# Linear attention and two gated layers on one core: joining tail tiles from the streamed copy, and two early attention loads

## The chip, the cores and the metric

The kernel runs on one core of a Trainium2 chip. A core has TensorE (matmuls, PE in the profile), VectorE (DVE), ScalarE (ACT), GpSimd (POOL) and SyncE (SP), which here only issues DMAs; ScalarE issues some DMAs too. Each engine works off its own list of instructions in order. The metric is the device time of one execution in microseconds (us), as a median of several runs; lower is better.

## The reference, cut to what matters

q, k and v are [8 batches, 8 heads, 576, 64] in float32. The weights of both layers are float64 arrays of [512, 2048] and [2048, 512].

```python
kv  = einsum('bhsd,bhse->bhde', k, v)
o   = einsum('bhsd,bhde->bhse', q, kv)
x   = o / sqrt(mean(o * o, -1) + 1e-6) * g_norm      # -> [4608 tokens, 512]
h   = x @ w_in1;  g = 0 if h <= -1, h if h >= 1, else (h + 1)**2 / 4;  x = g @ w_out1
h   = x @ w_in2;  g = max(h, 0)**2;                                    out = g @ w_out2
```

## The kernel before

**Numbers.** Every float32 factor is split into a high and a low part (`split`, `split_halves`), and a product is three matmuls (high by high, high by low, low by high). A split is a copy on ScalarE (the high part) and a subtraction on VectorE (the low part). A float64 weight arrives as pairs of 32-bit words and is first narrowed to float32 (`narrow_w`).

**Tokens.** They are cut into nine blocks of 512 (eight of the first 512 rows of each batch, one of what is left over). The first layer of blocks 0 to 4 (`PLAIN = 5`) runs plainly: 16 steps per block, one for each 128 columns f of the first matrix. In a step `h_stage` makes `ph` (12 matmuls), VectorE and ScalarE make `u` and its split `gs`, and two steps later `out_stage` adds it into four `acc` banks (12 matmuls). `ph` has two banks, so `ph` of step f+2 needs `u` of step f. Everything else goes in pairs of blocks by a Strassen scheme (`in_phase`, `out_phase`), which needs sums of quarters of the weight matrices.

**Preparation.** Those sums are made while the plain blocks run. A unit (which, i) does it for the column groups i and i+8 of matrix `which` (0 the first, 1 the second) of both layers. For layer 2 `prep_load` brings the raw weights, `prep_narrow`, `prep_sums` and `prep_split` make the parts. For layer 1 `prep_join` adds the high and low parts of tiles that already exist (`j` in the trace), and `prep_sums` and `prep_split` follow. Every split tile `s` is sent to DRAM (`wsd`) by a store that ScalarE issues a little later. The work is hung on half steps by `hook(s, ...)`: s = 32 b is the start of block b. There are 16 units, one every 8 half steps.

**Tail tiles.** The second matrix of layer 1 has 16 tiles of 512 KB. Tiles 0 to 6 stay on the chip. Tiles 7 to 15 (`TAIL = 9`) are kept in DRAM and streamed in every block from the second on, by `load_tail`, into a ring of three (`wt` in the trace): a load is issued when the matmuls on the tile three before it are done. The unit of the second matrix with number i needs tile i+8 as well (and tile 7 for i = 7). It loads a second copy of that tile, `wf`, by `prep_load` into a slot of a ring of four (`prep_tile`) that the split tiles `s` use too, and joins it in place.

**Hosted attention.** Attention of batches 5 to 7 runs beside other work. `EARLY` is batch 5, pairs 0 to 2, in block 4. `HOSTED[0]` is (6,0), (6,2), (5,3), (6,1), (6,3), placed in the slots of the first `in_phase`. A job is a load of keys and values (`load_kv`) and q (`load_q`), then `kv_stage` (`pkv` in the trace, 40 small matmuls for two pairs), `t_stage`, `o_stage` and `r_stage`.

**Order.** A scheduler builds each engine's list from the order in which the program issues the work. SP's list carries nearly all loads, so one load that waits for its slot holds the loads behind it.

Of the kernel before, what the change touches and what calls it, by code (L numbers as in the profile page):

```python
# [10 lines left out]
F32 = mybir.dt.float32  # L11
# [66 lines left out]
def linear_attention_rms_two_mlps(  # L78
# [12 lines left out]
    nc = tc.nc  # L91
# [3 lines left out]
    P = 128  # L95
    NP = H // 2
    KD = DM // P
    NF = DFF // P
# [15 lines left out]
    wp = ctx.enter_context(tc.tile_pool(name="wp", bufs=1))  # L114
    TAIL = 9
    RING = 3
    NH = NF // 2
    NQ = NH // 2
    H2 = P * 2
# [13 lines left out]
    PLAIN = 5  # L133
    PAIRS = [(2, 0), (1, PLAIN), (2, 2), (1, PLAIN + 2), (2, 4), (2, 6)]
    EARLY = ((5, 0), (5, 1), (5, 2))
    HOSTED = {
        0: ((6, 0), (6, 2), (5, 3), (6, 1), (6, 3)),
        2: ((7, 0), (7, 2), (7, 1), (7, 3)),
    }
    hosted = [a for n in HOSTED for a in HOSTED[n]]  # L140
# [151 lines left out]
    def kept_whole(L, which, f):  # L292
        return wsd[L, which, f % NH // 2][:, f // NH * 2 : f // NH * 2 + 2, f % 2]
# [13 lines left out]
    raw_tags = itertools.cycle((NF - TAIL + RING, NF - TAIL + RING + 1))  # L307
    prep_tags = itertools.cycle(range(NF - TAIL + RING + 2, NF))

    def prep_tile(name, shape, dtype):  # L310
        return wp.tile(shape, dtype, tag=f"w1_{next(prep_tags)}", name=name)

    prep = {}

    def prep_load(L, which, i):
        if L == 1:
            for n in range(2):
                f = i + n * NH
                if which == 1 and f >= NF - TAIL:
                    t = prep_tile(f"wf_{f}", [P, 2, 2, H2], F32)  # L320
                    nc.sync.dma_start(t, kept_whole(1, 1, f))
                    prep[L, which, i, n] = t
            return
        for f in (i, i + NH):
            t = wp.tile([P, 2 * TB], I32, tag=f"w1_{next(raw_tags)}", name=f"raw2_{which}_{f}")
            src = w_src[2][which]
            if which == 0:
                nc.sync.dma_start(
                    t.rearrange("p (c f) -> p c f", c=KD),
                    src[:, 2 * f * P : 2 * (f + 1) * P].rearrange("(c p) f -> p c f", p=P),  # L330
                )
            else:
                nc.sync.dma_start(t, src[f * P : (f + 1) * P, :])
            w_raw[2, f, which] = t.rearrange("p (f two) -> p f two", two=2)
# [76 lines left out]
    def load_kv(b, hp):  # L411
        h0 = 2 * hp
        if b > 0:

            r = rests[turn[b, hp] % len(rests)]
            kvr[b, hp] = (r[:, 0], r[:, 1])
        both = None
        if (b, hp) in hosted:
            both = kv_ring.tile([P, 2, TB], F32, f"kv_{b}_{hp}")
        for n, src in enumerate((k, v)):  # L420
            if both is not None:
                t = both[:, n, :]
            else:
                pool, tag = (ep, "e") if (b, hp) == (0, NP - 1) else (st, "st")
                t = pool.tile([P, TB], F32, tag=tag, name=f"{'kv'[n]}_{b}_{hp}")
            rows = src[b, h0 : h0 + 2, :TB, :].rearrange("h (p r) d -> p h r d", r=MR)
            if n == 0:

                t = t.rearrange("p (r h d) -> p r h d", h=2, r=MR)
                nc.sync.dma_start(t, rows.rearrange("p h r d -> p r h d"))  # L430
            else:
                t = t.rearrange("p (h r d) -> p h r d", h=2, r=MR)
                nc.sync.dma_start(t, rows)
            kvm.setdefault((b, hp), []).append(t)
            if b > 0:
                rest = src[b, h0 : h0 + 2, TB:, :].rearrange("h p d -> p h d")
                nc.sync.dma_start(kvr[b, hp][n][:REM], rest)
# [14 lines left out]
    def load_first():  # L452


        left = wp.tile([REM, 2, H, D], F32, tag="w0_7", name="kvr0")
        qr = wp.tile([REM, H, D], F32, tag="w1_6", name="qr0")
        for hp in range(NP):
            load_kv(0, hp)
            heads = slice(2 * hp, 2 * hp + 2)
            kvr[0, hp] = (left[:, 0, heads, :], left[:, 1, heads, :])  # L460
            pool, tag = (ep, "e") if hp == NP - 1 else (st, "st")
            t = pool.tile([P, TB], F32, tag=tag, name=f"q_0_{hp}")
            t = t.rearrange("p (c h d) -> p c h d", h=2, c=MR)
            rows = q[0, 2 * hp : 2 * hp + 2, :TB, :].rearrange("h (p c) d -> p c h d", p=P)
            nc.sync.dma_start(t, rows)
            qs[0, hp] = [t[:, c] for c in range(MR)] + [qr[:, heads, :]]
            if hp == 1:
                for f in range(2):
                    load_w(1, f, 0)
            if hp == 0:  # L470
                for d, src in ((left[:, 0], k), (left[:, 1], v), (qr, q)):
                    nc.scalar.dma_start(d, src[0, :, TB:, :].rearrange("h p d -> p h d"))
                for j in range(2):
                    nc.scalar.dma_start(
                        gvec[j * D : (j + 1) * D, :], g_norm.rearrange("(d o) -> d o", o=1)
                    )
# [177 lines left out]
    def attention(base, every, order):  # L654

        slots = []
        for j, (b, hp) in enumerate(order):
            s = base + int(every * j)
            turn.setdefault((b, hp), len(turn))
            if b == 1:  # L660
                slots += [(max(0, s - 7), load_kv, b, hp), (s, kv_stage, (b, hp))]
            elif j % 2 == 0:
                two = order[j : j + 2]
                turn.setdefault(two[-1], len(turn))
                slots += [(max(0, s - 7), load_kv, *i) for i in two]
                slots.append((s, kv_stage, *two))
            slots += [
                (max(0, s - 7), load_q, b, hp),
                (s, t_stage, b, hp),
                (s + 3, o_stage, b, hp, 0),  # L670
                (s + 4, o_stage, b, hp, 1),
            ]
            if j == 0 and b < PLAIN:
                slots.append((s + 6, begin, b))
            slots.append((s + 6, r_stage, b, hp))
        if b < PLAIN:
            slots.append((2 * NF * b, store_xrem, b))
        return slots
# [425 lines left out]
    def hook(s, f, *a):  # L1104
        hooks.setdefault((s // 2, s % 2), []).append((f, a))
# [19 lines left out]
    for j, (w, f) in enumerate(kept):  # L1125
        hook(14 + 2 * j, keep_first, w, f)

    for j in range(2 * NH):
        which, i = j % 2, j // 2
        s0 = 2 * NF - 1 + 8 * j  # L1130
        for d, L, f, a in (
            (-6, 2, prep_load, ()),
            (0, 2, prep_narrow, (0,)),
            (1, 2, prep_narrow, (1,)),
            (2, 2, prep_sums, ()),
            (2, 2, prep_split, (0,)),
            (3, 2, prep_split, (1,)),
            (3, 2, prep_split, (2,)),
            (4, 2, prep_split, (3,)),
            (4, 1, prep_load, ()),  # L1140
            (6, 1, prep_join, ()),
            (7, 1, prep_sums, ()),
            (7, 1, prep_split, (2,)),
            (8, 1, prep_split, (3,)),
        ):
            hook(s0 + d, f, L, which, i, *a)

    last = 2 * (PLAIN - 1) * NF
    first_x = x2_jobs(0, Ring(*[(st, "st")] * 7))
# [4 lines left out]
        hook(last + t, load_w2)  # L1154
    in_pair = {}
    for n in HOSTED:
        for s, *job in sorted(attention(3, 6.5 if n == 0 else 7, HOSTED[n]), key=lambda j: j[0]):
            in_pair.setdefault((n, s), []).append(job)

    nc.scalar.preload_act_table_set("natural_log_exp_and_others")  # L1160
    load_first()
# [14 lines left out]
    for j in range(2):  # L1176
        s = slice(j * D, (j + 1) * D)
# [140 lines left out]
```

## Time and profile before

| what | value |
|---|---|
| median of 3 runs | 1588.13 us (1586.63 to 1588.62) |
| the profiled execution | 1591.16 us, span 1589.4 us |
| TensorE busy | 1545.9 us, 97% of the span |
| VectorE, ScalarE busy | 1197.8 us (75%), 930.4 us (59%) |
| DMA | 392.36 MB, mean 247 GB/s |

The profiled execution took 1591.16 us, of which the span that the profiler shows is 1589.4; both are a little above the median of the other runs. "Busy" is time in which an engine executes; a row of idle time names what ended the wait.

### The profile page before, as it was taken

How to read it: one execution, taken by the hardware profiler on the slowest of the kernel's cores; microseconds unless marked ns; L12 is line 12 of the kernel's file. 1: busy time of each engine (PE TensorE's matmuls, PEld its weight loads, DVE VectorE, ACT ScalarE, POOL GpSimd, SP SyncE). 2: the span in 40 equal slices, each digit the busy share in tenths (PEclk: the TensorE clock that was granted, in tenths of full speed). 3: DMA queues.
4: the chain of work that ended last, by engine and by line, in shares of the span. 5: the costliest groups of instructions: out<-in, count | busy, mean ns of one | idle time of the engine just before them, and what ended most of it. 6: DMA issues, size and time to landing. Idle time of an engine off the chain costs nothing.

```text
span 1589.4 us, 22383 instructions
## 1 busy us (share of the span) xinstructions
PE 1545.9 (97%) x7633; PEld 1271.6 (80%) x7633; DVE 1197.8 (75%) x2112; ACT 930.4 (59%) x1751; POOL 13.1 (1%) x30
## 2 busy tenths in 40 slices
PE   9999799999998889999999999999999999999999
PEld 5787687778876778888888888788888888888899
DVE  6975787887968847896888478878884587559666
ACT  5976665667756636764765366546753454346354
POOL 0000000000000000000000000000000000000000
PEclk9999999999999989999999999999999999999999
DMA  9676999889897887778777867687777676977796
GB/s 293 195 238 193 320 311 309 258 272 314 256 313 239 280 253 202 239 217 217 226 242 224 265 197 238 213 228 239 247 219 221 197 243 196 243 241 216 224 387 251
DMA packets 333090, 392.36 MB, mean 247 GB/s; under 512 B 197936, under 2 KB 223536, under 8 KB 332976
## 3 DMA queue, kind: packets, MB, share of 16 engines
q1 hardware_dynamic: 302080, 334.82, 69.9%
q10 hardware_dynamic: 30896, 56.11, 9.5%
q8 instruction: 61, 1.00, 0.2%
q14 instruction: 53, 0.43, 0.1%
HBM read 304.61 MB, written 86.25 MB: 246 GB/s over the span
## 4 chain that ended last, share of the span: by engine, by line
PE 82%; DVE 7%; DMA 7%; ACT 4%; issue 1%; SPq 0%; ACTq 0%; DVEq 0%
PE ph L881 30%; PE po L881 30%; PE acc L243 9%; PE ph L243 8%; DMA wsd<-s 3%; DMA wf<-wsd 1%; DMA wt<-wsd 1%; PE po L243 1%; PE pkv L490 1%; PE pr L612 1%; DVE s L190 1%; DVE t L810 1%; DVE u L708 1%; PE pwarm L1171 1%; DVE x L810 1%
## 5 line engine op out<-in xcount | busy, mean ns | idle before, releaser
L881 PE MATMUL ph<-x,ws 128*128 128x512 f32 (+1 forms) x2352 | 505.5, 375 | 0.9 <-DVE u L708 0.5
L881 PEld LDWEIGHTS ph<-x,ws 128*128 128x128 f32 x2352 | 418.1, 189 | 79.2 <-DVE e L937 0.8
L881 PE MATMUL po<-t,ws 128*128 128x512 f32 x2016 | 460.9, 390 | 0.3 <-DVE t L810 0.2
L881 PEld LDWEIGHTS po<-t,ws 128*128 128x128 f32 x2016 | 377.4, 188 | 81.0 <-DVE t L810 2.8
L810 DVE TENSOR_TENSOR t<-g,t 128x512 fp32r<-128x512 f32 (+1 forms) x336 | 215.9, 649 | 87.2 <-ACT t L222 84.6
L222 ACT CAST t<-g 128x512 fp32r<-128x512 f32 (+1 forms) x336 | 195.7, 590 | 116.4 <-PE po L881 58.6
L243 PE MATMUL ph<-x,w 128*128 128x512 f32 x960 | 245.8, 400 | 16.4 <-DVE u L708 14.8
L243 PEld LDWEIGHTS ph<-x,w 128*128 128x128 f32 x960 | 179.1, 191 | 60.2 <-DVE u L708 19.7
L243 PE MATMUL acc<-gs,w 128*128 128x512 f32 x528 | 135.7, 396 | 5.4 <-DVE gs L235 3.5
L958 ACT ACTIVATE g<-h 128x512 f32<-128x512 f32 (+1 forms) x120 | 70.7, 589 | 88.1 <-DVE h L947 88.0
L243 PEld LDWEIGHTS acc<-gs,w 128*128 128x128 f32 x528 | 97.9, 190 | 26.4 <-DVE gs L235 3.9
L937 DVE TENSOR_TENSOR e<-ph,e 128x512 f32<-128x512 f32 (+1 forms) x112 | 72.1, 650 | 58.6 <-PE ph L881 55.5
L243 PE MATMUL acc<-gs,wt 128*128 128x512 f32 x432 | 110.4, 403 | 2.1 <-DMA wt<-wsd 1.8
L947 DVE CUSTOM_DVE_ANT_0 h<-ph,e 128x512 f32<-128x512 f32 (+1 forms) x120 | 76.3, 637 | 47.4 <-PE ph L881 43.4
L243 PEld LDWEIGHTS acc<-gs,wt 128*128 128x128 f32 x432 | 83.6, 196 | 20.6 <-ACT u L229 2.2
L222 ACT CAST x<-xr 128x512 fp32r<-128x512 f32 (+1 forms) x98 | 57.5, 590 | 50.5 <-DVE xr L861 29.2
L222 ACT CAST gs<-u 128x512 fp32r<-128x512 f32 x80 | 49.9, 624 | 46.3 <-DVE u L708 29.6
L235 DVE TENSOR_TENSOR gs<-u,gs 128x512 fp32r<-128x512 f32 x80 | 54.8, 685 | 21.8 <-ACT gs L222 21.7
L708 DVE SCALAR_TENSOR_TENSOR u<-u,ph 128x512 f32<-128x512 f32 x80 | 54.5, 681 | 16.1 <-ACT u L229 15.8
L934 ACT COPY e<-ph 128x512 f32<-128x512 f32 (+1 forms) x56 | 30.8, 554 | 58.5 <-PE ph L881 51.6
L706 ACT ACTIVATE u<-ph,halfb 128x512 f32<-128x512 f32 x80 | 55.3, 691 | 13.4 <-PE ph L243 10.0
L810 DVE TENSOR_TENSOR x<-xr,x 128x512 fp32r<-128x512 f32 (+1 forms) x98 | 62.8, 646 | 0.0
(135 smaller groups left out, 1623.9 us busy)
## 6 DMA issues: line engine op xcount, KB each, us to landing
ws<-wsd SPq DMA_DIRECT2D x392, 512.0 KB, 4.1
wsd<-s ACTq DMA_DIRECT2D x96, 512.0 KB, 5.4
wt<-wsd SPq DMA_DIRECT2D x36, 512.0 KB, 5.8
raw<-in_moe_w_in_dram SPq DMA_DIRECT2D x32, 512.0 KB, 6.4
raw<-in_moe_w_out_dram SPq DMA_DIRECT2D x32, 512.0 KB, 5.7
xr<-x1d SPq DMA_DIRECT2D x36, 256.0 KB, 4.9
out_dram<-ov SPq DMA_DIRECT2D x142, 64.0 KB, 3.6
wsd<-w SPq DMA_DIRECT2D x17, 512.0 KB, 4.4
```

The costliest lines, as they stand in the source:

```text
L190: lo.tensor_tensor(t[:, :, 1, :], src, t[:, :, 0, :].bitcast(F32), ALU.subtract)
L222: return e.copy(dst, src)
L235: lo = engine(op + "_lo", phase).tensor_tensor(t[:, 1, :], src, t[:, 0, :].bitcast(F32), ALU.subtract)
L243: nc.tensor.matmul(dst, wt(a), xt(c), start=first and n == 0, stop=last and n == 2)
L706: nc.scalar.activation(u, ps, AF.Relu, bias=halfb, scale=0.5)
L708: nc.vector.scalar_tensor_tensor(u, u, 1.0, ps, op0=ALU.min, op1=ALU.max)
L810: engine2(op + "_lo").tensor_tensor(t[:, 1, :], src, t[:, 0, :].bitcast(F32), ALU.subtract)
L881: nc.tensor.matmul(ps, wt(a), xt(c), start=first and n == 0 and i == 0, stop=last and n == len(lhs) - 1 and i == 2, skip_group_check=True,)
L934: nc.scalar.copy(e[i, 1], bank)
L937: nc.vector.tensor_tensor(e[i, p], bank, e[i, 1], ALU.add)
L947: nc.vector._custom_dve(TENSOR_ADD_SAT, out=h, in0=bank, in1=add, s0=float("inf"), s1=0.0)
L958: nc.scalar.activation(g, h, AF.Square)
```

## The change

It has three parts. First, the units are put in another order: block n+1 now gets the units (0, 2n), (0, 2n+1), (1, n) and (1, n+4), at 32(n+1) - 4 + 2n + 0, 8, 16, 24 half steps; the last one starts one half step earlier, and what would fall behind block 4 is put in its last half step. By that order the second-matrix unit i meets the streamed tile i+8 of the same block, and `prep_join` reads that tile (into a small tile `j`) in place of a copy of its own. Only tile 7 of the last unit is still loaded as `wf`, into a slot of the ring for raw weights. Second, keys, values and q of the first two hosted pairs, (6,0) and (6,2), are loaded from half step 25 of block 4, the keys and values into the ring `st` (names `k_`, `v_`) and no longer into `kv_ring` (`kv_`). Third, the first hosted attention starts in slot 1 of the first `in_phase`, before in slot 3.

```diff
     def prep_load(L, which, i):
         if L == 1:
-            for n in range(2):
-                f = i + n * NH
-                if which == 1 and f >= NF - TAIL:
-                    t = prep_tile(f"wf_{f}", [P, 2, 2, H2], F32)
-                    nc.sync.dma_start(t, kept_whole(1, 1, f))
-                    prep[L, which, i, n] = t
+            if which == 1 and i >= NF - TAIL:
+                t = wp.tile([P, 2, 2, H2], F32, tag=f"w1_{next(raw_tags)}", name=f"wf_{i}")
+                nc.sync.dma_start(t, kept_whole(1, 1, i))
+                prep[L, which, i, 0] = t
             return
...
-        if (b, hp) in hosted:
+        if (b, hp) in hosted[2:]:
             both = kv_ring.tile([P, 2, TB], F32, f"kv_{b}_{hp}")
...
-    for j in range(2 * NH):
-        which, i = j % 2, j // 2
-        s0 = 2 * NF - 1 + 8 * j
+    units = []
+    for n in range(NQ):
+        for which, i, s in ((0, 2 * n, 0), (0, 2 * n + 1, 8), (1, n, 16), (1, n + NQ, 24)):
+            units.append((which, i, 2 * NF * (n + 1) - 4 + 2 * n + s))
+    units[-1] = (*units[-1][:2], 2 * NF * PLAIN - 7)
+    for which, i, s0 in units:
...
-            (4, 1, prep_load, ()),
+            (2, 1, prep_load, ()),
...
-            hook(s0 + d, f, L, which, i, *a)
+            hook(min(s0 + d, 2 * NF * PLAIN - 1), f, L, which, i, *a)
...
-        for s, *job in sorted(attention(3, 6.5 if n == 0 else 7, HOSTED[n]), key=lambda j: j[0]):
-            in_pair.setdefault((n, s), []).append(job)
+        for s, *job in sorted(attention(3 if n else 1, 7 if n else 6.5, HOSTED[n]), key=lambda j: j[0]):
+            if n == 0 and s == 0 and job[0] in (load_kv, load_q):
+                hook(last + 25, *job)
+            else:
+                in_pair.setdefault((n, s), []).append(job)
```

Three places in the engines' lists show it. In the names the numbers are block and step (`u_2_6` is `u` of block 2, step 6), tile (`wt_9`), or matrix and unit; the last number is a running one.

VectorE, block 2, where a second-matrix unit is joined; before:

```order
L708 SCALAR_TENSOR_TENSOR u_2_6_2983<-u_2_6_2983,ph_2_6_2970 128x512
L235 TENSOR_TENSOR gs_2_6_2989<-u_2_6_2983,gs_2_6_2989 128x512
L346 TENSOR_TENSOR wf_2967<-wf_2967 128x2x256
L366 TENSOR_TENSOR s_1_1_2_3087<-j_2_3024,wf_2967 128x256
L369 TENSOR_TENSOR s_1_1_2_3087<-s_1_1_2_3087,j_2_3024 128x256
```

and with the change:

```order
L706 SCALAR_TENSOR_TENSOR u_2_9_3197<-u_2_9_3197,ph_2_9_3184 128x512
L596 TENSOR_TENSOR s2lo_2_3208<-wk_3_2_3080,s_3_2_3168 128x576
L190 TENSOR_TENSOR s_1_1_3_3210<-s_2_1_1_3140,s_1_1_3_3210 128x2x256
L344 TENSOR_TENSOR j_9_3270<-wt_9_3176 128x512
L365 TENSOR_TENSOR s_1_1_1_3299<-j_1_3268 128x256
L364 TENSOR_TENSOR s_1_1_1_3298<-j_1_3268,j_9_3270 128x256
```

The join that read a private copy `wf` behind step 6 now reads the streamed tile `wt_9` behind step 9.

SP, end of block 4, the loads for the first hosted pairs; before:

```order
L303 DMA wt_14_5537<-wsd_1_3_113 128x2x512
L430 DMA kv_0_5659<-in_k_dram 128x8x64
L433 DMA kv_0_5659<-in_v_dram 128x2x256
...
L303 DMA wt_15_5584<-wsd_1_3_113 128x2x512
...
L430 DMA kv_2_5664<-in_k_dram 128x8x64
L321 DMA wf_5542<-wsd_1_3_113 128x2x512
L321 DMA wf_5544<-wsd_1_3_113 128x2x512
L433 DMA kv_2_5664<-in_v_dram 128x2x256
```

and with the change:

```order
L428 DMA k_0_5474<-in_k_dram 128x8x64
...
L303 DMA wt_10_5268<-wsd_1_1_111 128x2x512
L431 DMA v_0_5477<-in_v_dram 128x2x256
L428 DMA k_2_5480<-in_k_dram 128x8x64
...
L795 DMA ws_0_0_7_5085<-wsd_0_0_114 128x1024
L431 DMA v_2_5483<-in_v_dram 128x2x256
...
L303 DMA wt_13_5455<-wsd_1_2_112 128x2x512
...
L319 DMA wf_5546<-wsd_1_3_113 128x2x512
```

Three of the four loads of keys and values moved ahead of tile 11, the fourth (`v_2`) ahead of tile 13; one `wf` is left, behind tile 15.

TensorE, end of block 4, where `pkv` of the hosted pairs stands; before:

```order
L490 MATMUL pkv_0_5773<-kv_0_5659 64x64 x8
...
L243 MATMUL ph_4_15_5592<-x_4_0_3815,w_0_15_1154 128x512 x3
...
L490 MATMUL pkv_0_5773<-kv_2_5664 64x64 x8
```

and with the change:

```order
L243 MATMUL acc_4_3_4798<-gs_4_12_5440,wt_12_5394 128x512 x3
L488 MATMUL pkv_0_5706<-v_0_5477,k_0_5474 64x64 x8
L488 MATMUL pkv_0_5706<-rest_130 64x64 x2
L488 MATMUL pkv_0_5706<-v_2_5483,k_2_5480 64x64 x8
L488 MATMUL pkv_0_5706<-rest_129 64x64 x2
L243 MATMUL ph_4_15_5600<-x_4_0_3806,w_0_15_1154 128x512 x3
```

The part of the second pair moved up, from behind `acc` of step 14 to in front of `ph` of step 15.

## Rows read from the trace of the kernel before

**Rows 1.** The page, busy time of the engines.

```profile
PE 1545.9 (97%) x7633; PEld 1271.6 (80%) x7633; DVE 1197.8 (75%) x2112; ACT 930.4 (59%) x1751; POOL 13.1 (1%) x30
```

**Rows 2.** Windows: length, busy time (instructions) per engine, granted clock, DMA share, GB/s.

```profile
160.00:200.00 40.00, 30.59 (x160) 24.10 (x159) 31.11 (x60) 25.56 (x50) 0.81 (x2) 0.91 0.99 321
560.00:600.00 40.00, 36.02 (x164) 29.80 (x165) 19.69 (x35) 17.37 (x36) 0.00 (x0) 0.87 0.78 240
1100.00:1200.00 100.00, 100.00 (x443) 82.81 (x442) 81.50 (x131) 59.72 (x98) 0.00 (x0) 1.00 0.73 229
```

**Rows 3.** Timeline of TensorE: start, length, instructions, [idle before, what ended it].

```profile
170.34 5.43 PE L243 MATMUL ph<-x,w 128*128 128x512 f32 x12 [5.80 <-DVE u L708]
246.65 4.58 PE L243 MATMUL acc<-gs,wt 128*128 128x512 f32 x12 [1.81 <-DMA wt<-wsd]
272.08 2.88 PE L243 MATMUL acc<-gs,w 128*128 128x512 f32 x12
300.35 0.69 PE L490 MATMUL pkv<-v,k 128*64 128x64 f32 x16 [2.06 <-DVE t L530]
301.66 4.61 PE L243 MATMUL ph<-x,w 128*128 128x512 f32 x12
353.23 3.02 PE L243 MATMUL ph<-x,w 128*128 128x512 f32 x12 [1.69 <-DVE u L708]
451.41 3.01 PE L243 MATMUL ph<-x,w 128*128 128x512 f32 x12 [1.33 <-DVE u L708]
503.85 1.22 PE L243 MATMUL acc<-gs,w 128*128 128x512 f32 x2 [3.54 <-DVE gs L235]
528.44 3.01 PE L243 MATMUL ph<-x,w 128*128 128x512 f32 x12 [2.11 <-DVE u L708]
548.32 0.69 PE L490 MATMUL pkv<-kv 128*64 128x64 f32 x16 [2.06 <-DMA kv<-in_v_dram]
563.49 1.12 PE L490 MATMUL pkv<-kv 128*64 128x64 f32 x16 [4.62 <-DMA kv<-in_k_dram]
565.32 2.92 PE L881 MATMUL ph<-x,ws 128*128 128x512 f32 x6 [0.49 <-DVE u L708]
568.04 3.85 PE L243 MATMUL acc<-gs,wt 128*128 128x512 f32 x9
```

**Rows 4.** Timeline of VectorE: two `u` of block 1, two joins of `wf`, block 4's end.

```profile
150.51 0.69 DVE L708 SCALAR_TENSOR_TENSOR u<-u,ph 128x512 f32<-128x512 f32 x1 [0.43 <-ACT u L229]
169.61 0.68 DVE L708 SCALAR_TENSOR_TENSOR u<-u,ph 128x512 f32<-128x512 f32 x1
297.52 0.69 DVE L346 TENSOR_TENSOR wf<-wf 128x512 f32<-128x512 f32 x1 [4.96 <-DMA wf<-wsd]
502.50 0.69 DVE L346 TENSOR_TENSOR wf<-wf 128x512 f32<-128x512 f32 x1 [6.29 <-DMA wsd<-s]
545.68 0.65 DVE L861 TENSOR_TENSOR xr<-xr,xr 128x512 f32<-128x512 f32 x1
546.25 0.68 DVE L708 SCALAR_TENSOR_TENSOR u<-u,ph 128x512 f32<-128x512 f32 x1
```

**Rows 5.** All joins of the copy `wf`: idle time of VectorE before them.

```profile
  DMA wf<-wsd: 23.7, 5
  DMA wsd<-s: 6.3, 1
  DMA rest<-in_v_dram: 4.8, 1
```

**Rows 6.** Waits of SP's queue: total us, times, longest.

```profile
SPq L321 <- DMA wsd<-s: 17.7, 6, 5.4
```

**Rows 7.** DMA issues: count, KB each, median us from issue to landing.

```profile
wt<-wsd SPq DMA_DIRECT2D x36, 512.0 KB, 5.8
v<-in_v_dram SPq DMA_DIRECT2D x23, 256.0 KB, 4.9
```

**Rows 8.** The chain that ended last: one tail tile's transfer in block 1.

```profile
234.26 12.25 DMA wt<-wsd
```

## The prediction

> **What bounds the kernel now.** I start from the page: TensorE is busy for 1545.9 us of a span of 1589.4 [rows 1], so it sets the pace, and all that can be won without taking matmuls away is the 43.5 us in which it stands, and the stretches in which it runs at half its clock. The windows say where these lie. In the Strassen part (1100 to 1200 us) TensorE is busy all the time and the granted clock is 1.00; in the plain blocks there are windows of 40 us with 30.59 busy, and with a clock of 0.91 and 0.87 [rows 2]. So the timeline of TensorE is read for its idle times, one by one [rows 3]. [...]
>
> Then the reasons. Most rows name VectorE (`u`, `gs`, `t`), so VectorE's own waits are read. In front of the joins of the private copy `wf` it stood for 23.7 + 6.3 + 4.8 us [rows 5], 4.96 at 297 us and 6.29 at 502 us [rows 4]. These lead to TensorE's idle times at 300 (2.06), 353 (1.69), 451 (1.33) and 503 us (3.54): what TensorE waits for stands in VectorE's list behind such a join. And why was `wf` late? SP waited 17.7 us in six of the nine cases until the store of a split tile had freed the slot [rows 6]; only then did the transfer begin. The wait at 548 us and that at 563 us are for values and keys of the first hosted pairs themselves, which SP issues late, the second between the last two `wf`.
>
> **The change part by part.** All against the profiled execution, 1591.2 us.
>
> *Eight of nine loads of `wf` go.* With them go SP's waits for the slot, and VectorE's for the transfer. What TensorE lost behind these: at 300 us 2.06 + (4.61 - 2.88) = 3.8; at 353 us 1.7; at 451 us 1.3; at 503 us 3.5 [rows 3]. Together 10.3.
>
> *Hosted keys, values and q early.* The waits at 548 us (2.1) and 563 us (4.62, 0.49, then 2.92 for six in place of 1.44 and 3.85 for nine in place of 2.16, so 4.62 + 0.49 + 1.48 + 1.69 = 8.3) go: 10.4. The last `wf` pair, for which VectorE stood here too, becomes one load behind the last tail tile, in a slot of the raw ring, which its unit's narrowing frees.
>
> *What follows from these.* At 528 us 2.11 are waited for a `u` behind work that VectorE has piled up since the wait at 502 us; bounds 0 and 2.1, I take 1.0. At 246 us a tail tile needed 12.25 us [rows 8] while the next `wf` moved beside it at a DMA share near 1 (0.99 in the window before, [rows 2]); bounds 0 and 1.81 + 1.70 = 3.5, I take 1.0, since the copy was issued 5 us behind the tile. Removed in all: 10.3 + 10.4 + 2.0 = 22.7 us.
>
> *The joins now wait for streamed tiles.* A tail load is issued when the tile three before it is done, that is about one step (two times 2.88 us) ahead of the join's place in the list and two ahead of its matmuls. The median transfer is 5.8 us [rows 7], about that lead, so I take 0; bounds 0 and what the longest transfer would cost, under the rivals. What hides the join is then the step in between; without it VectorE's list stands still, and `u` with it.
>
> *A new wait in front of `ph` of step 15.* `pkv` of both pairs now stands there on TensorE. Three of its four loads are issued many steps ahead. The fourth, values of (6,2), gets the slot in `st` of a tile whose last reader is the last difference of x quarters (`xr`, L861 before); in the changed list that stands right behind `u` of step 13. Before, `u` of step 13 was done at 546.9 us [rows 4], when TensorE came to the same place (548.32 less 2.06: 546.3). The load then lands 4.9 us later [rows 7], and TensorE would stand for some 5.5 us, with the clock 8.6. But VectorE comes there earlier: it lacks the 6.29 us wait at 502 us, while TensorE lacks 3.54 and about 1.0; and in the changed list some 4 us of preparation (part of the last unit, which starts two half steps later, and a transpose) stand behind `u` of step 13 and no longer before. That is some 5.5 us less. Bounds 0 and 8.6; I take 3.0, since the estimate of what VectorE is ahead may be half wrong. Behind that load on SP are tail tiles 13 and 14, needed one and two steps later, so they are covered.
>
> *The units in other places.* VectorE has the same operations, but in other bunches. At the opening of block 1, the list before has 26 rows between `u` of step 3 and of step 4, which took from 151.2 to 169.6 us [rows 4] and cost TensorE 5.80 and (5.43 - 2.88) [rows 3], 8.4 in all. The changed list has a bunch of 32 rows, between `u` of steps 4 and 5, but two `gs` lie in the midst of it, and `u` of step 4 comes early. At the same pace it takes 4.2 us more; bounds -8.4 (no stall) and +4.2; I take 0. In block 4 the fullest two steps have 28 rows in place of 25, and blocks 2 and 3 get their bunches at other steps. A bunch that is a little too long costs what the small waits cost now, 1.3 to 1.7 us [rows 3]; bounds 0 and two in each of blocks 2 to 4 with the dearer figure, 10; I take one each, 4.5.
>
> *Sum.* 1591.2 - 22.7 + 0 + 3.0 + 0 + 4.5 = 1576.0 for a profiled execution. The median of the runs lies 3.0 below the profiled one, so **1573 us**. The bounds together (all good, all bad) give some 1591.2 - 20.7 - 5.6 - 8.4 - 3.0 = 1553 and 1591.2 - 20.7 + 8.6 + 4.2 + 10 - 3.0 = 1590.
>
> [...] The page shows TensorE at 97%, VectorE at 75% [rows 1]. [...]
>
> **The rivals.**
>
> *Hidden anyway, 1587 (within 0.2%).* TensorE is the engine that is full, and VectorE has as much to do as before (75%). Then each wait that goes comes back at the next bunch: VectorE is no longer held at 502 us, but the bunches at 170, 353 and 451 us are there in the new lists as well, and 20.7 us are given back as stalls of 1.3 to 5.8 each. For it: at 503 to 550 us VectorE worked with hardly a gap and TensorE still waited at 528 us. Against it: at 300 and 503 us VectorE itself stood idle for 4.96 and 6.29 us right before [rows 4]; that is no lack of capacity.
>
> *The values come late, 1580.* The load behind the difference of x costs its full 8.6 us in place of 3.0: 1573 + 5.6 = 1579, and with a step of TensorE waiting for tail tile 13 behind it about 1580. It is so if VectorE's lag at step 13 is the old one. For it: the rows at 545.68 and 546.25 us. Against it: the working above.
>
> *The joins wait, 1595 (slower).* Eight joins in the four blocks wait on VectorE for a streamed tile. If transfers take what the one at 234 us took, 12.25 us [rows 8], a join one step (5.8 us) behind the issue stands for 6.5 us, eight of them 52. Of the 34.8 us of idle time before `wf` [rows 5] TensorE lost 10.3 plus the 8.3 at 563 us, about half; so 26 us against the 20.7 that go: 1588 + 26 - 20.7 = 1593, and 1595 with a half-clock stretch. It decides from a mean wait of 5 us per join on, a landing of 11 us. Against it: the median is 5.8 us of 36 such transfers, and TensorE, which needs the same tiles a step later, waited for one only once, 1.81 us.
>
> **How the numbers follow.** The forecast, stalls behind `wf` and at the end of block 4 gone, 1562 to 1578: 0.66. Late values or dearer bunches, 1578 to 1584: 0.15. Hidden, 1585 to 1591: 0.10. Slower through the joins or the bunch of block 1, above 1591: 0.07. Better than 1562: 0.02. The range 1562 to 1587 leaves out about 0.02, 0.07 and half of the hidden case. This kernel's measurement tells a difference of about 0.2%, 3.2 us: faster 0.83, same 0.09, slower 0.08.
>
> **What would show it.** In the profile after, the groups of VectorE's waits should have one `wf` join left, and joins of `wt` without 5 us of idle time before them; TensorE's idle rows at the places of 300, 353, 451 and 503 us should be gone, and those in front of `pkv` at the end of block 4 be one, under 4 us, ended by a load of values. Block 1 should still have its stall of several us, one or two steps later. I am wrong if joins of `wt` show waits, if `pkv` waits over 6 us, or if the windows of blocks 2 to 4 show as much idle TensorE as now with VectorE busy.

## The result and the profile after

The changed kernel takes 1570.47 us (median of 4 runs, 1569.12 to 1574.38), beside 1588.38 for the kernel before on the same chip: a ratio of 0.9892 [0.9873, 0.9912], 17.9 us less. Its profiled execution took 1570.57 us with a span of 1568.8, that of before 1591.16.

The page of the changed kernel, its line of busy times [rows 1 for before]:

```profile
PE 1537.6 (98%) x7631; PEld 1268.9 (81%) x7633; DVE 1197.7 (76%) x2112; ACT 932.2 (59%) x1751; POOL 11.9 (1%) x30
```

TensorE stood for 31.2 us of the span (1568.8 less 1537.6), before for 43.5. The rest of the 20.6 us between the two spans is clock: the mean granted clock is 0.996 in place of 0.990, and TensorE's "busy" time for the same matmuls is 8.3 us less. The windows of the changed kernel (the columns as in [rows 2]):

```profile
160.00:200.00 40.00, 34.62 (x175) 27.11 (x174) 34.55 (x66) 27.54 (x57) 0.94 (x2) 0.91 0.99 308
240.00:480.00 240.00, 234.10 (x1195) 192.56 (x1194) 194.25 (x368) 165.67 (x331) 4.25 (x8) 0.99 0.86 272
520.00:560.00 40.00, 35.57 (x189) 28.68 (x189) 28.53 (x54) 21.17 (x41) 0.00 (x0) 1.00 0.97 300
560.00:600.00 40.00, 40.00 (x219) 33.35 (x218) 30.35 (x50) 25.95 (x52) 0.00 (x0) 1.00 0.71 218
```

The window from 560 us, which had stood at a clock of 0.87, is full and at a clock of 1.00. That at 160 us still has the clock of before, 0.91. TensorE's idle times behind 160 us in the changed kernel, from its timeline (those over 1 us; the columns as in [rows 3]):

```profile
171.51 2.10 PE L243 MATMUL acc<-gs,w 128*128 128x512 f32 x8 [2.21 <-DVE gs L235]
...
174.71 0.53 PE L243 MATMUL po<-qT,kvbd 128*128 128x288 f32 x2 [1.09 <-ACT qT L222]
...
176.84 1.33 PE L243 MATMUL po<-qT,kvbd 128*128 128x288 f32 x4 [1.60 <-DVE qT L569]
...
415.24 0.53 PE L243 MATMUL po<-qT,kvbd 128*128 128x288 f32 x2 [1.64 <-ACT qT L222]
...
472.93 0.53 PE L243 MATMUL po<-qT,kvbd 128*128 128x288 f32 x2 [3.50 <-ACT qT L222]
473.30 4.48 PE L243 MATMUL ph<-x,w 128*128 128x512 f32 x12
...
517.17 0.53 PE L610 MATMUL pr<-s2lo,ones 128*128 128x288 f32 x2 [1.44 <-DVE s2lo L596]
...
542.70 1.66 PE L879 MATMUL ph<-x,ws 128*128 128x512 f32 x6 [2.36 <-DVE u L706]
...
552.32 8.01 PE L879 MATMUL ph<-x,ws 128*128 128x512 f32 x34 [2.07 <-ACT ev L743]
...
636.36 0.53 PE L243 MATMUL po<-qT,kvbd 128*128 128x288 f32 x2 [1.93 <-ACT qT L222]
```

All waits of [rows 3] from 246 us on are gone; between 240 and 390 us there is no wait of 0.3 us or more. But there are new ones, at 415, 473, 517, 542, 552 and 636 us, of which that at 473 us costs 3.50 and 1.6 more (twelve matmuls in 4.48 in place of 2.88, at a granted clock of 0.62 from 473.3 to 477.8 us). What ScalarE, VectorE and the queue in which ScalarE issues its stores did before that wait:

```profile
471.27 0.37 ACTq L182 DMA_DIRECT2D wsd<-s  x1
471.69 0.63 ACT L229 ACTIVATE u<-u 128x512 f32<-128x512 f32 x1 [4.55 <-DMA xr<-x1d]
```
```profile
472.35 0.69 DVE L706 SCALAR_TENSOR_TENSOR u<-u,ph 128x512 f32<-128x512 f32 x1 [3.87 <-ACT u L229]
```

ScalarE stood for 4.55 us until it had issued a store, and VectorE stood behind it for 3.87; so this wait doesn't come from a full VectorE. VectorE's waits in front of joins, in the list of waits (total, times, longest):

```profile
DVE j L344 <- DMA wt<-wsd: 6.9, 4, 2.3
```

Four joins of streamed tiles wait, 6.9 us in all, where the private copies had cost 34.8 [rows 5]. SP's wait for the slot of a copy [rows 6] is gone.

### The profile page after: what moved, and what is told of

It reads as the page before. It is cut to its first block, busy times and chain, and to the rows that moved or that the text cites. A ratio compares the mean times of both kernels' runs of the same rounds, so it can differ in the third digit from the quotient of the medians.

```text
span 1568.8 us, 22366 instructions
## 1 busy us (share of the span) xinstructions
PE 1537.6 (98%) x7631; PEld 1268.9 (81%) x7633; DVE 1197.7 (76%) x2112; ACT 932.2 (59%) x1751; POOL 11.9 (1%) x30
## 4 chain that ended last, share of the span: by engine, by line
PE 77%; DMA 6%; DVE 2%; ACT 2%; SPq 0%; issue 0%; ACTq 0%; DVEq 0%
PE po L879 32%; PE ph L879 31%; PE ph L243 6%; PE acc L243 6%; DMA wsd<-s 3%; DMA wt<-wsd 1%; PE po L243 1%; DMA ws<-wsd 1%; PE pkv L488 1%; PE pr L610 1%; DMA rest<-in_v_dram 1%; DMA xr<-x1d 1%; DMA xr<-xpd 0%; ACT s L222 0%; DVE s L190 0%
## 5 line engine op out<-in xcount | busy, mean ns | idle before, releaser
L243 PE MATMUL acc<-gs,w 128*128 128x512 f32 x528 | 131.7, 394 | 4.5 <-DVE gs L235 2.2
L243 PE MATMUL acc<-gs,wt 128*128 128x512 f32 x432 | 106.2, 391 | 0.8 <-DMA wt<-wsd 0.8
L243 PEld LDWEIGHTS acc<-gs,wt 128*128 128x128 f32 x432 | 79.9, 188 | 17.6 <-DMA wt<-wsd 1.2
L235 DVE TENSOR_TENSOR gs<-u,gs 128x512 fp32r<-128x512 f32 x80 | 54.9, 686 | 20.8 <-ACT gs L222 20.6
```

Of the source, the lines that this page charges most:

```text
L235: lo = engine(op + "_lo", phase).tensor_tensor(t[:, 1, :], src, t[:, 0, :].bitcast(F32), ALU.subtract)
L243: nc.tensor.matmul(dst, wt(a), xt(c), start=first and n == 0, stop=last and n == 2)
```

## The experiments

Each has its own runs of the kernel before on the same chip, so ratios are compared. "The changed kernel" stands at 0.9892.

**1. Only the units.** Hosted loads and start as before.

```diff
-        if (b, hp) in hosted[2:]:
+        if (b, hp) in hosted:
...
-        for s, *job in sorted(attention(3 if n else 1, 7 if n else 6.5, HOSTED[n]), key=lambda j: j[0]):
-            if n == 0 and s == 0 and job[0] in (load_kv, load_q):
-                hook(last + 25, *job)
-            else:
-                in_pair.setdefault((n, s), []).append(job)
+        for s, *job in sorted(attention(3, 6.5 if n == 0 else 7, HOSTED[n]), key=lambda j: j[0]):
+            in_pair.setdefault((n, s), []).append(job)
```

> Only the new unit order and the joins from streamed tiles; the hosted keys, values and q are loaded where they were, and the first hosted attention starts in slot 3 as before. Theory (two separate groups of waits, about 10 us behind the private copies and about 8 to 10 us in front of the small key-value matmuls at the end of block 4): the first group goes, the second stays, 1578 to 1580 us, and the rows of TensorE at 500 us and before have no wait for a join of a private copy, while the matmuls of keys and values still wait for a load. Rival A (the units are all of it): 1571. Rival B (the early loads are all of it): 1588.

1567.18 us, 0.9869 [0.9854, 0.9885]. That is rival A, and no less than the whole change. At the end of block 4 its timeline of TensorE has one wait for a hosted load left:

```profile
532.26 1.12 PE L488 MATMUL pkv<-kv 128*64 128x64 f32 x16 [2.16 <-DMA kv<-in_v_dram]
```

The pair (6,2), for which TensorE had stood 4.62 us and more at 563 us [rows 3], is in time, though its loads are hung where they were. So the theory of two separate groups of waits fell.

**2. The early loads without the units:** the kernel before with the last block of the change's diff, so with its start in slot 1 too, and `hosted[2:]`.

> The kernel before with only the early loads of the first two hosted pairs and the start in slot 1; units, order and private copies as before. Theory: the waits in front of the key-value matmuls at the end of block 4 go, those behind the private copies at 300, 353, 451 and 503 us stay: 1578 to 1581 us; the two parts then add up to the whole change. Rival A (the units are all of it): 1588. Rival B (the early loads are all of it): 1571.

1588.55 us, 1.0007 [0.9996, 1.0018]: nothing, for the two parts together. The waits in front of `pkv` did go; what came is in the timelines of TensorE and VectorE of this kernel:

```profile
506.56 0.80 PE L243 MATMUL acc<-gs,w 128*128 128x512 f32 x1 [5.58 <-DVE gs L235]
...
562.88 0.61 PE L243 MATMUL po<-qT,kvbd 128*128 128x288 f32 x1 [3.25 <-ACT qT L222]
...
656.29 0.53 PE L243 MATMUL po<-qT,kvbd 128*128 128x288 f32 x2 [1.38 <-ACT qT L222]
```
```profile
503.84 0.69 DVE L346 TENSOR_TENSOR wf<-wf 128x512 f32<-128x512 f32 x1 [6.43 <-DMA wf<-wsd]
...
560.14 0.69 DVE L346 TENSOR_TENSOR wf<-wf 128x512 f32<-128x512 f32 x1 [3.20 <-DMA wf<-wsd]
...
564.59 0.69 DVE L346 TENSOR_TENSOR wf<-wf 128x512 f32<-128x512 f32 x1 [2.10 <-DMA wf<-wsd]
```

TensorE now waits at the end of block 4 for `qT`, whose work stands on VectorE and ScalarE around the join of the last pair of copies. Without the keys' wait the copies' own wait is what ends last. The wait at 656 us, with a clock of 0.89 from 650 to 665 us, is not in the kernel before; it comes with the start in slot 1 (experiment 7). So this run gives the sum of the two parts, and what the early loads alone are worth in the old order was not measured.

**3. The change with the private copies kept.** The old `prep_load`, hung at 4 half steps.

```diff
-            if which == 1 and i >= NF - TAIL:
-                t = wp.tile([P, 2, 2, H2], F32, tag=f"w1_{next(raw_tags)}", name=f"wf_{i}")
+            for n in range(2):
+                f = i + n * NH
+                if which == 1 and f >= NF - TAIL:
+                    t = prep_tile(f"wf_{f}", [P, 2, 2, H2], F32)
...
-            (2, 1, prep_load, ()),
+            (4, 1, prep_load, ()),
```

> The changed kernel, with the unit order and the early loads, but the units of the second matrix load their private copy of the tail tile again (nine loads of 512 KB into the slots that the split tiles use) and join that. Theory (the private copy, its wait for a slot in SP's list and VectorE's wait for it are what cost): some 10 us come back, 1578 to 1582, with waits of VectorE of 4 us and more in front of joins of the copy. Rival (the places of the units are what gains, the copy is harmless): 1571, within 2 us of the changed kernel.

1604.67 us, 1.0104 [1.0089, 1.012]. More than expected came back, 34 us over the changed kernel: in the new order the copies cost more than in the old (21.2 us, experiment 5). Of its list of waits and of VectorE's timeline:

```profile
DVE wf L346 <- DMA wf<-wsd: 46.2, 7, 10.5
```
```profile
343.69 0.69 DVE L346 TENSOR_TENSOR wf<-wf 128x512 f32<-128x512 f32 x1 [9.33 <-DMA wf<-wsd]
```

**4. The copies loaded but not read.** As 3, but the joins take the streamed tiles. There are seven such loads, not the eight of the expectation (the last unit has none).

```diff
+            elif which == 1:
+                t = prep_tile(f"wx_{i}", [P, 2, 2, H2], F32)
+                nc.sync.dma_start(t, kept_whole(1, 1, i + NH))
```

> As the kernel with the private copies kept, eight loads of 512 KB into the same slots at the same places, but nobody reads them: the joins take the streamed tiles, as in the changed kernel (tile 7 of the last unit apart). The loads are then only traffic and a place in SP's list that waits for a slot. Theory (what costs is that VectorE's list stands still behind the join): 1571 to 1574, at most 3 us above the changed kernel. Rival C (SP's list that stands still, or the traffic, makes streamed tiles and other loads late, and that is the cost): 1577 or more, and waits of TensorE or VectorE for streamed tiles.

1575.23 us, 0.9922 [0.9904, 0.994]: 4.8 us over the changed kernel, with the same slots. SP's waits for them and VectorE's for joins:

```profile
SPq L323 <- DMA wsd<-s: 6.3, 4, 4.4
```
```profile
DVE j L347 <- DMA wt<-wsd: 7.4, 4, 3.1
```

Between the theory's 3 and the rival's 7; the intervals of this and the changed kernel overlap. SP's waits for the slots were much the same in experiment 3, 7.0 us. So of the 34 us some 29 come only when VectorE's joins read the copies (nine there, seven loads here), and some 5, not clear of the noise, from the traffic and SP's place.

**5. The old order without copies.** The nine joins read tiles that lie on the chip, so the sums of those tiles are other ones.

```diff
-            for n in range(2):
-                f = i + n * NH
-                if which == 1 and f >= NF - TAIL:
-                    t = prep_tile(f"wf_{f}", [P, 2, 2, H2], F32)
-                    nc.sync.dma_start(t, kept_whole(1, 1, f))
-                    prep[L, which, i, n] = t
...
-                w = (wi[L, f] if which == 0 else wo[L, f]).bitcast(F32)
+                w = (wi[L, f] if which == 0 else wo[L, f if f < NF - TAIL else f % (NF - TAIL)]).bitcast(F32)
```

> The kernel before with its own unit order and its own hosted loads, but no private copy at all: the nine joins of tail tiles read a tile that lies on the chip (tile 1 for 8, 2 for 9 and so on), so the sums of these tiles are of other values; the work of VectorE is the same. Theory (the private copies are what cost, in either order; the 8.3 us in front of the key-value matmuls at 563 us were theirs as well, since the loads stood behind the last pair of copies in SP's list): 3.8 + 1.7 + 1.3 + 3.5 + 8.3 = 18.6 us go, about 1569 to 1573. Rival (the new order gains by itself, a better spread of VectorE's work): 1578 or more.

1565.61 us, 0.9858 [0.9837, 0.988], 21.2 us less than before. The rival falls: the order itself gains nothing. (Nine transfers are gone with them; in experiment 4 seven unread ones cost some 5 us.) Its window of blocks 2 to 4, and behind it the same window of the kernel before:

```profile
240.00:480.00 240.00, 239.67 (x1219) 197.54 (x1219) 200.53 (x380) 169.02 (x341) 3.29 (x8) 1.00 0.90 287
```
```profile
240.00:480.00 240.00, 230.94 (x1157) 187.51 (x1156) 190.08 (x361) 159.93 (x321) 6.15 (x8) 0.99 0.90 285
```

With the old list of VectorE and no copy to wait for, TensorE loses 0.3 us in 240; the changed kernel, in the new order, loses 5.9 there (the window above). What is left of this kernel's end of block 4 and of its block 1:

```profile
170.01 4.59 PE L243 MATMUL ph<-x,w 128*128 128x512 f32 x12 [5.04 <-DVE u L702]
...
198.94 2.47 PE L243 MATMUL acc<-gs,wt 128*128 128x512 f32 x5 [4.13 <-DMA wt<-wsd]
...
528.28 0.69 PE L484 MATMUL pkv<-kv 128*64 128x64 f32 x16 [1.60 <-DMA kv<-in_v_dram]
541.02 0.69 PE L484 MATMUL pkv<-kv 128*64 128x64 f32 x16 [2.20 <-DMA kv<-in_v_dram]
```

The two waits for hosted loads are 3.8 us here, 10.4 in the kernel before; both loads and starts are as before. So 6.6 of the 10.4 belonged to the copies: 2.9 of waits, the rest clock and the 0.49 behind.

**6. Joins two half steps sooner,** `(4, 1, prep_join, ())` for `(6, ...)`.

> The changed kernel with each unit's join two half steps (one step of TensorE, 5.8 us) earlier in the lists, half a step behind the issue of the tile's load in place of one and a half. Theory (a join that meets its tile too early holds VectorE's list, as the private copies did): eight joins wait some 4 to 6 us each, about half of it reaches TensorE, 1585 to 1595. Rival (VectorE has slack for it, since TensorE is the full engine): 1571, within 3 us of the changed kernel.

1573.03 us, 0.9906 [0.9888, 0.9923]. It doesn't tell the theories apart, since the scheduler put the joins in VectorE's list behind the same `u` as in the changed kernel (only that of the last unit moved, by one row). The rival that joins wait was thus not tried beyond the waits that the changed kernel has.

**7. Early loads, start in slot 3.** The changed kernel with `attention(3, ...)` for `attention(3 if n else 1, ...)`.

> The changed kernel with the hosted attention started in slot 3 as before; only the early loads of keys, values and q stay as changed. The kernel with the units alone took 1567.2, the changed one 1570.5. If the start in slot 1 is what loses the 3 us (its VectorE work meets the last unit and the first difference tiles): 1567. If the early loads lose them (transfers beside the last tail tiles): 1570 to 1571.

1565.46 us, 0.9862 [0.9843, 0.9881]. The waits at 552 us (2.07) and 636 us (1.93 and 0.51) are not in its timeline, that in front of `ph` is:

```profile
541.26 2.08 PE L879 MATMUL ph<-x,ws 128*128 128x512 f32 x6 [2.75 <-DVE u L706]
543.14 4.12 PE L243 MATMUL acc<-gs,wt 128*128 128x512 f32 x12
```

So the start in slot 1 loses some 4.5 us by these rows, and the clock falls behind the wait at 636 us too (0.87 from 630 to 640 us, here 1.00). That wait, 1.9 to 2.4 us in two pieces, is in the traces of all kernels that start in slot 1 (2, 3, 4 and 6 as well, at 637 to 671 us) and of none that starts in slot 3. The one at 552 us is less certain: in experiment 6 it is 0.35. The early loads lose nothing that shows against experiment 1, and gain nothing clear of the noise. The intervals of this kernel and of the changed one still touch, so the loss is read from the traces and not shown by the times.

**8. Stores by GpSimd,** in the kernel of experiment 1: `nc.gpsimd.dma_start(dst, src)` for `nc.scalar.dma_start(dst, src)` in `pay`.

> The kernel with the units alone (1567.2), with the stores of split tiles and of x1 quarters issued by GpSimd, which is idle, in place of ScalarE. Theory (what is left at 175, 416 and 473 us, 3.4 us at the longest, is ScalarE's list standing in the issue of a store): these rows go, 1560 to 1564. Rival (the transfers themselves are late in a full DMA, whoever issues them): 1567. A third: GpSimd issues later or more slowly, slots come free later, 1570 and more.

1586.11 us, 0.9993 [0.9979, 1.0006], the third way. The table of DMA issues of this kernel (xcount, KB, median us to landing) and a row of its list of waits; behind them the same of experiment 1:

```profile
wsd<-s POOLq DMA_DIRECT2D x96, 512.0 KB, 6.6
```
```profile
ACT s L222 <- DMA wsd<-s: 24.3, 11, 4.1
```
```profile
wsd<-s ACTq DMA_DIRECT2D x96, 512.0 KB, 5.2
```
```profile
ACT s L222 <- DMA wsd<-s: 12.9, 7, 2.9
```

A store lands later (6.6 us against 5.2), and ScalarE waits twice as long (24.3 us against 12.9) to write a split tile into a slot that such a store must free. That this is all of the 19 us is not shown: the scheduler made other lists, and VectorE's joins wait longer than in the changed kernel (6.9):

```profile
DVE j L344 <- DMA wt<-wsd: 12.8, 3, 7.2
```

**9 and 10. Two attempts at the waits that are left,** on the kernel of experiment 7: the first differences of x quarters two to four half steps later (9), the units of block 1 two half steps later (10).

```diff
-    when = [2, 3, 3, 4, 5, 6, 7, 8, 7, 9, 9, 10, 11, 12, 13, 14]
+    when = [2, 4, 5, 5, 6, 7, 8, 9, 7, 9, 10, 11, 12, 13, 14, 15]
```
```diff
-            units.append((which, i, 2 * NF * (n + 1) - 4 + 2 * n + s))
+            units.append((which, i, 2 * NF * (n + 1) - (2 if n == 0 else 4) + 2 * n + s))
```

> The kernel with the units and the early loads but the start in slot 3 (0.9862 of before, 1565.5), with the first differences of x quarters, which begin in block 4, hung two to four half steps later. What is to go is the row at 472 us (2.27 to 3.5 us and a stretch at half clock; ScalarE stands there in the issue of a store while the x quarters move and the DMA share is 1.0). If VectorE's bunch there (18 rows between two u) and those transfers are the cause: 1561 to 1563. If the store is slow for another reason: 1565. If the later differences collide with the end of block 4: 1568.

> The same kernel with the units of block 1 hung two half steps later. VectorE's longest bunch there, 33 rows between u of step 4 and step 5, falls apart into bunches of 7 to 15. Theory (the stall of 5.2 us at 170 to 179 us and the half clock behind it come from that bunch, not from the transfers): 5.2 us and 3 to 4 us of half clock go, 1557 to 1560. Rival (the transfers of the raw weights and the store that ScalarE issues hold it, DMA share 0.99): 1564 to 1566.

9 took 1565.63 us (0.9865 [0.9843, 0.9887]), 10 took 1565.89 (0.987 [0.985, 0.9889]): both the same as experiment 7. Single traces scatter: up to 440 us the lists of TensorE, VectorE and SP in 9 are those of 7, yet TensorE is busy for 71.21 us at a clock of 0.94 from 160 to 240 us, there 71.89 at 0.98. In 9 the wait at 472 us fell to 0.37, but others of 0.96 and 0.65 came at 498 and 513. In 10 the waits of 171 to 179 us went, and these came (TensorE's timeline):

```profile
193.00 0.73 PE L243 MATMUL ph<-x,w 128*128 128x512 f32 x2 [1.93 <-DVE u L706]
198.90 4.60 PE L243 MATMUL acc<-gs,wt 128*128 128x512 f32 x12 [1.72 <-DMA wt<-wsd]
213.86 5.46 PE L243 MATMUL acc<-gs,wt 128*128 128x512 f32 x12 [3.34 <-DMA wt<-wsd]
```

**11. The copy sooner,** in the kernel before: `(2, 1, prep_load, ())` for `(4, ...)`.

> The kernel before with each private copy hung two half steps earlier and, in the ring of slots, behind the first split tile of its unit in place of the last, so that it takes a slot that is freed earlier. The joins move up in VectorE's list by up to a step as well. Theory A (it is SP's wait for the slot that makes the copy late): the waits in front of the joins shrink to a third and the time is 1570 to 1576. Theory B (a copy of 512 KB beside the raw weights and tail tiles is late wherever it is issued, and the join in the list goes with it): 1585 to 1595.

1580.27 us, 0.9953 [0.9939, 0.9967], between the two. The lists of waits of VectorE and of SP (for before see [rows 5, 6]):

```profile
DVE wf L346 <- DMA wf<-wsd: 13.6, 4, 4.7
```
```profile
SPq L321 <- DMA wsd<-s: 1.9, 2, 1.5
```

SP's wait fell from 17.7 to 1.9 us, VectorE's from 34.8 to 13.6, the time by 8.4. So issuing the copy earlier, into a slot that is freed earlier, took away a good part of its lateness; the two weren't tried apart. What holds the time up is not shown to be the transfer alone, since ScalarE now waits longer for the slots of split tiles (11.7 before):

```profile
ACT s L222 <- DMA wsd<-s: 26.0, 14, 5.8
```

**12. First-layer stores closer together,** on the kernel of experiment 7: `hook(14 + 5 * j // 4, keep_first, w, f)` for `14 + 2 * j`.

> The kernel with the units, the early loads and the start in slot 3 (0.9862 of before), with the stores of the first layer's own tiles hung closer together, so that they end in the middle of block 1's first third and not at its end: some 14 transfers of 256 KB leave the stretch 160 to 235 us, where the DMA share is 1.0, for 80 to 160 us, where it is 0.36 to 0.83. The scheduler also makes VectorE's longest bunch of block 1 25 rows in place of 33. When the units of block 1 alone were moved, TensorE's wait of 5.2 us at 171 us came back as 7 us of waits at 193 to 214, five of them for tail tiles. Theory (in block 1 the transfers are the limit, and a stall that is moved comes back while they are): 1557 to 1561. Rival (VectorE's bunches are the limit in block 1, wherever the transfers lie): 1564 to 1567.

1573.65 us, 0.9909 [0.9889, 0.993]: worse, and neither theory had it. Its timeline of TensorE:

```profile
148.42 1.90 PE L243 MATMUL ph<-x,w 128*128 128x512 f32 x5 [2.50 <-DVE u L706]
177.80 2.50 PE L243 MATMUL ph<-x,w 128*128 128x512 f32 x5 [3.35 <-DVE u L706]
```

The stall of block 1 is there, in other places and one of them earlier. What sets block 1's loss stays open.

## Why the prediction was right, and where its steps were not

The forecast was 1573 us, the time is 1570.5; the sum for the profiled execution was 1576.0, it took 1570.6. The mechanism that the sum rests on, VectorE's list standing behind a join for a private copy, is shown by experiments 3 to 5. But several terms were wrong, and their errors nearly cancel: the copies were worth about twice what was booked for them, the early loads hardly anything, and three costs were off in both directions. That 1573 came so near is in part luck.

*Eight loads of `wf` go, 10.3.* The right cause, too small. Without any copy, in the old order, 21.2 us go. The 10.3 counted the four rows behind which `wf` visibly stood. It left out 6.6 us of the next term, the waits of 0.34 to 1.33 us between 472 and 492 us (3.2 in all, of which experiment 5 has 0.55), and the clock at 503 us: the row there has two matmuls in 1.22 us, and the granted clock from 500 to 510 us is 0.83 (0.50 from 503.8 to 505.1), some 1.7 us more.

*Hosted loads early, 10.4.* This step failed. It took the waits at 548 and 563 us as due to where the loads are hung. With the start in slot 1 the early loads gained nothing in the old order (experiment 2); with the units alone the waits shrank to 2.16 (experiment 1), and beside them the early loads gained nothing clear of the noise (experiment 7 against 1). The prediction had the fact in hand ("the second between the last two `wf`"): SP issued the values of (6,2) behind two copies, and its third rival books the 8.3 us to `wf`. In experiment 5, where they are not, the two waits cost 3.8. So some 6.6 of the 10.4 should have been booked to the copies; what became of the other 3.8 is not shown.

*The start in slot 1,* costed at nothing without a reason, loses some 4.5 us by the rows at 552 and 636 us that experiment 7 doesn't have. At 552 us what TensorE waits for stands on VectorE and ScalarE, which are also at work on the first hosted attention; the prediction looked only at its loads.

*What follows, 2.0.* Both rows, at 246 and 528 us, are gone: up to 5.6.

*Joins of streamed tiles, 0.* Close: 6.9 us of VectorE's idle time, of which TensorE felt 1.44 at 517 us, right behind the join that waited for 2.29. The other long one, 2.28 at 405 us, lies 10 us ahead of the wait at 415 us (1.64), with VectorE at work in between; that it caused it is not shown. "Without 5 us of idle time before them" held. The rival that the joins wait (1595) didn't come; how near it is wasn't tried, since experiment 6 left the joins in place; in experiment 8, where the stores land later, one join waits for 7.2 us.

*The new `pkv` wait, 3.0.* Wrong: it is 0. `pkv` of both pairs runs at 529.22 us without a wait. SP and VectorE of the changed kernel:

```profile
512.89 0.38 SPq L431 DMA_DIRECT2D v<-in_v_dram  x1
```
```profile
526.83 0.68 DVE L706 SCALAR_TENSOR_TENSOR u<-u,ph 128x512 f32<-128x512 f32 x1
527.42 0.68 DVE L859 TENSOR_TENSOR xr<-xr,xr 128x512 f32<-128x512 f32 x1
```

The last early values were issued at 512.89, 15 us ahead of the difference of x quarters that was to free their slot. So the values didn't wait for that difference; the step had the wrong last reader of that slot.

*Block 1, 0.* Its waits are 2.21, 1.09, 1.60 and 0.34, so 5.2 against 5.80 in one piece and 3.6 more at 198 us, and the clock still falls (0.91 from 160 to 200 us, as before). The stretch 160 to 240 us has 72.69 us of TensorE at 0.96, before 70.59 at 0.94. Two traces with the same lists there differ by nearly as much (71.21 at 0.94 in experiment 9), so no gain is shown, and 0 holds.

*Bunches of blocks 2 to 4, 4.5.* Too small, and only in part of that cause: the rows from 415 to 542 us add up to 1.64 + 3.50 + 1.6 + 1.44 + 2.36 = 10.5, about the upper bound. But 5.1 of it, at 473 us, is no bunch of VectorE: VectorE stood idle for 3.87 us there, behind ScalarE. Moving the differences of x quarters took most of this wait away (0.37 in experiment 9). With the old list and no copies TensorE lost 0.3 us in the 240 us in which it now loses 5.9 (experiment 5). So in these blocks the new order costs something, and it is there to read the streamed tiles; by itself it gains nothing.

*The rivals.* "Hidden anyway" was wrong for the copies: VectorE stood idle for 34.8 us in front of their joins [rows 5], and without them 21.2 us went (experiment 5). It was right for what merely moves work in experiments 9 and 10: they took waits of 1.9 and 4.9 us away, others came elsewhere, and the time stayed. TensorE, the busiest engine (97% before), is the one that gained, from 43.5 us of idle time to 31.2, though the cause stood in the list of an engine that is busy for 75%.

The changed kernel has not the lowest median of these. Two kernels with the new units that leave the first hosted attention in slot 3 are lower, 0.9869 (experiment 1) and 0.9862 (experiment 7), with intervals that touch its own; the simplest is the units alone.

## What to carry to other kernels

When a wait disappears from the place where it was read, ask whose it was: follow the late load back in its queue to what stands ahead of it, and book the wait there. Price apart a transfer that is only traffic (some 5 us here) and the same transfer with an instruction waiting for it in a shared in-order list (29 us more). A change of three parts needs each part alone: here one gave all; the other two were first tried together, and that run couldn't tell a part that gains nothing from one whose gain the other loses.

## What was not expected of the hardware

In the changed kernel TensorE stood for 2.36 us at 542 us, and the six matmuls behind it took 1.66 us at a granted clock of 1.00 (half of the 2.88 that twelve take would be 1.44); in experiment 7 it stood 2.75 us at the same place, the six took 2.08, and the twelve behind took 4.12 in place of 2.88, at a granted clock of 0.83 from 540 to 550 us, in the changed kernel 1.00. So two waits that differ by 0.4 us cost 2.6 and 4.6 us (2.36 and 0.2; 2.75, 0.6 and 1.2). In experiment 10 it stood 2.69 us there and the six took 1.65, and at 300 us in the kernel before the twelve matmuls behind a wait of 2.06 took 4.61 [rows 3] at a granted clock of 0.64 (301.6 to 306.3 us), so in these runs the length of the wait alone doesn't tell it. And 96 stores of 512 KB and 20 of 256 KB, handed from ScalarE to a GpSimd that is busy for 1% in the changed kernel, made the kernel 19 us slower (1567.18 to 1586.11).
